# Attention weights turned in 32x32 squares on VectorE and placed by DMA through DRAM, in place of TensorE transposes

## The chip, the cores and the metric

The kernel runs on one core of a Trainium2 chip. The metric is the device time of one execution in microseconds (us), as the median of several runs; lower is better.

## What is computed

Eight batches of causal attention with a window of 128 keys and a linear distance bias, followed by a feed-forward layer with a squared Relu:

```python
B, H, S, D = 8, 8, 576, 64
scores = (q @ k^T) / sqrt(D)                     # per batch and head
rel = pos[:, None] - pos[None, :]
mask = (rel >= 0) & (rel < 128)
scores = where(mask, scores - slope[h] * abs(rel), -1e9)
attn = softmax(scores)                           # divided by (sum + 1e-9)
x = (attn @ v) as [4608 tokens, 512]             # heads side by side
h = maximum(x @ w_in, 0)                         # w_in 512 x 2048
out = (h * h) @ w_out                            # w_out 2048 x 512
```

Inputs and output are float32.

## The kernel before

The 4608 tokens are cut into nine chunks of 512. A chunk's attention has eight **segments**: four pairs of heads times two halves of 256 tokens. Segment k belongs to chunk k // 8, to the pair of heads k // 2 % 4 and to half k % 2. A segment's weights stand in a tile `t` of 128 x 4 x 128: 128 partitions are two blocks of 64 queries, the middle index m is a head and a half of the segment, and the last one is a ring of 128 keys.

The feed-forward layer of a chunk has 16 steps f. In each, `gemm1` (line 169) makes 128 hidden rows by 12 matmuls into one PSUM bank `g`, ScalarE takes the Relu (line 178) into `r`, VectorE squares it (line 184), ScalarE rounds it to `hh` (line 186) and VectorE keeps the rest in `hl` (line 188); two steps later `gemm2` (line 199) adds 12 more matmuls into four accumulators `acc`. There is one buffer of `r` and one bank of `g`.

The first two chunks' attention, and the first GEMM, are laid out by `start` with a planner. From segment 18 on, two segments (a **couple**, q = 9 to 35) are handled together, and the GEMMs of the chunk before run between their parts. TensorE's order is the order in which the code is written. The loop at line 702 counts half steps t (even: gemm1, odd: gemm2), and a couple has 8 of them:

- at part 0 the couple before is finished by `both` (line 352): two times 16 matmuls of weights with values (`mix`, line 335) into one bank, split into high and low parts `xu` by ScalarE and VectorE (lines 359 and 360). The next couple's loads of qk and v are put on SyncE's queue. Then `front`: the couple's scores (line 414), the copy and the mask (lines 441 to 464), the row's maximum (276), the exponential (283), sums and reciprocal (290, 291), and the normalisation on GpSimd (294).
- at parts 3 and 5 `middle` turns one segment each: `turn` has four TensorE transposes of 128 x 128 against the identity into PSUM (line 302), `out` copies them to `own` (ScalarE, line 309), and `before` and `same` make from it, by a select on GpSimd, the part of the ring that belongs to earlier keys (`prev`, line 312) and that of the same block (`own`, line 318).

`own` and `prev` are the two halves of one buffer of the pool `pp`, which has two buffers, so a couple fills both, and a new one is free when the couple before has been mixed. Segments 16 and 17 (couple 8) are scored and normalised in `start`; segment 16 is turned there too, segment 17 in the loop. All engines but TensorE get their order from a scheduler that simulates the program. Each engine, and SyncE's queue with the loads and stores, works through its own list in order.

Of the kernel before, what the change touches and what calls it, by code (L numbers as in the profile page):

```python
# [9 lines left out]
F32 = mybir.dt.float32  # L10
# [4 lines left out]
ALU = mybir.AluOpType  # L15
# [31 lines left out]
class Kern:  # L47
    def __init__(self, ctx, tc, qkd, vd, w1d, w2d, cstd, outd):
        self.tc, self.nc = tc, tc.nc
        self.qkd, self.vd = qkd, vd  # L50
        self.w1d, self.w2d, self.cstd, self.outd = w1d, w2d, cstd, outd
        ep = lambda name, bufs, **kw: ctx.enter_context(tc.tile_pool(name=name, bufs=bufs, **kw))
        self.c = ep("const", 1)
        self.ld = ep("ld", 3)
        self.tp = ep("tp", 3)
        self.pp = ep("pp", 2)
        self.sm = ep("sm", 6)
        self.xu = ep("xu", 8)
        self.hp = ep("hp", 3)
        self.op = ep("op", 4)  # L60
        self.sc = ep("sc", 1, space=PSUM)
        self.at = ep("at", 1, space=PSUM)
        self.g1 = ep("g1", 1, space=PSUM)
        self.ac = ep("ac", 4, space=PSUM)
        self.cst = self.c.tile([128, CST], F32, name="cst")
        self.ident = self.cst[:, 0:128]
        self.mask = self.cst[:, 128:192].bitcast(I32)
        self.never = self.cst[:, 192:256]
        self.raw, self.w = [None] * NF, [None] * NF
        self.nc.alloc_sbuf_tensor("arena", [128, NF * 2048], F32)  # L70
        self.arena = self.nc.sbuf_base - NF * 8192
        self.x, self.qk, self.v, self.h, self.segs = {}, {}, {}, {}, {}
        at = lambda slot, name, shape: self.nc.alloc_sbuf_tensor_at(name, shape, F32, offset=self.arena + slot * 4096).ap()
        self.wide = [at(2 * (NF - 3), "wide", [128, H, 256])[:, 2 * p : 2 * p + 2] for p in range(NP)]
        self.room_t = [at(2 * (NF - 5) + n, f"tw{n}", [128, 4, 256]) for n in range(4)]
        self.start_banks = [self.ac.tile([128, 512], F32, name="acc") for _ in range(4)]
# [138 lines left out]
class Segment:  # L215
# [133 lines left out]

    def both(self, other):
        K = self.K
        X = K.at.tile([128, 512], F32, name="at")
        for s in (self, other):
            s.X = X[:, 256 * s.sg : 256 * s.sg + 256]
            s.mix(s.sg == 0)
        u = K.x[self.c, self.p] = K.xu.tile([128, 2, 512], F32R, name="xu")
        self.nc.scalar.copy(u[:, 0], X)
        self.nc.vector.tensor_tensor(u[:, 1], X, u[:, 0].bitcast(F32), op=ALU.subtract)  # L360
# [5 lines left out]
        self.sums()  # L366
        self.norm()

    def middle(self):
        self.turn()  # L370
        self.out()
        self.before()
        self.same()


class Couple:
# [218 lines left out]
def start(K):  # L595
# [31 lines left out]
    for k in range(18):  # L627
        G = K.segs[k] = (Wide if k < 8 else Segment)(K, k)
        c, p, sg = G.c, G.p, G.sg
        n = lambda s, *m: (s, k, *m)  # L630
        after = [("q", c, p, 0), ("q", c, p, 1)][: sg + 1] + ([("s", k - 1)] if k else []) + LATER * (k == 8)
        chain = lambda s: ((s, k - 1),) if k else ()
        if k < 8:
            d, slot, w = 4.0 * k, "sa" if k % 2 else "sc", 0.75 if G.skip else 1.0
            P.add(n("s"), "PE", 0.9 * w, tuple(after), d, G.scores, slot)
            for m in range(4):
                P.add(n("u", m), "DVE", 0.35 * w, (n("u", m - 1) if m else n("s"), ("k", p)), d + 0.5, do(G.top, m), None if m else "tw", slot if m == 3 else None)
                P.add(n("e", m), "Activation", 0.48 * w, (n("u", m),) + ((n("e", m - 1),) if m else ()), d + 0.5, do(G.exp, m))
            P.add(n("r"), "DVE", 0.4, (n("e", 3),), d + 1, G.sums)
            P.add(n("n"), "Pool", 2.05 * w, (n("r"),), d + 1, G.norm)  # L640
            P.add(n("z"), "PE", 0.9 * w, (n("n"),) + chain("z"), d + 1, G.turn, ("at", "zp", "pp"), "tw")
            P.add(n("o"), "Activation", 0.6, (n("z"),), d + 1, G.out, None, "at")
            P.add(n("m"), "DVE", 0.62 if w == 1 else 0.36, (n("z"),), d + 1, G.also, None, "zp")
            P.add(n("x"), "PE", 1.0, (n("m"), n("o"), ("v", c, p)) + chain("x"), d + 2, G.values, "xa", "pp")
            P.add(n("h"), "Activation", 0.4, (n("x"),), d + 2, G.high)
            P.add(n("l"), "DVE", 0.36, (n("h"),), d + 2, G.low, None, "xa")
        else:
            d = RING(k)
            P.add(n("s"), "PE", 0.9, tuple(after), d, G.scores, "sc")
            P.add(n("b"), "Activation", 0.6 if not G.late else 0.8, (n("s"),), d, G.base, "t")  # L650
            P.add(n("f"), "DVE", 0.7 if not G.late else 1.1, (n("b"),), d, G.fold, None, "sc")
            for m in range(4):
                P.add(n("t", m), "DVE", 0.22, (n("t", m - 1) if m else n("f"), "nrel"), d + 0.5, do(G.top, m))
                P.add(n("e", m), "Activation", 0.4, (n("t", m),) + ((n("e", m - 1),) if m else ()), d + 0.5, do(G.exp, m))
            P.add(n("r"), "DVE", 0.4, (n("e", 3),), d + 1, G.sums)
            P.add(n("n"), "Pool", 1.05, (n("r"),), d + 1, G.norm)
            if k > 16:
                continue
            P.add(n("z"), "PE", 0.55, (n("n"),) + chain("z"), d + 1, G.turn, ("at", "pp"), "t")
            P.add(n("o"), "Activation", 0.6, (n("z"),), d + 1, G.out, None, "at")  # L660
            P.add(n("p"), "Pool", 0.72, (n("o"),), d + 1.5, G.before)
            P.add(n("m"), "Pool", 0.66, (n("p"),), d + 1.5, G.same)
            if k > 15:
                continue
            P.add(n("x"), "PE", 1.1, (n("m"), ("v", c, p)) + chain("x"), d + 2, G.values, "at", "pp")
            P.add(n("h"), "Activation", 0.4, (n("x"),), d + 2, G.high)
            P.add(n("l"), "DVE", 0.36, (n("h"),), d + 2, G.low, None, "at")
        if sg == 1:
            P.add(n("ld"), "free", 0.0, (n("x"),), d + 2, None, None, None if (c, p) == (0, 3) else "ld")
# [24 lines left out]
@with_exitstack  # L694
def tile_attn_moe(ctx: ExitStack, tc: tile.TileContext, *aps):
    K = Kern(ctx, tc, *aps)
    K.const()
    with tc.manual_schedule(engines={ENGINES["PE"]}):
        with tc.manual_schedule(engines={e for n, e in ENGINES.items() if n != "PE"}):
            start(K)  # L700
        pairs = {8: (K.segs[16], K.segs[17])}
        for n in range(NF, NF * NCH + 2):
            for t in (2 * n, 2 * n + 1):
                q, part = divmod(t - FIRST, 8)
                q += 9
                with tc.high_priority(offset=50):
                    if part == 0:
                        if q - 1 in pairs:
                            first, second = pairs.pop(q - 1)
                            first.both(second)  # L710
                        if q + 1 < 4 * NCH:
                            K.load(*divmod(q + 1, 4))
                        if q < 4 * NCH:
                            C = Couple(K, q)
                            C.front()
                            pairs[q] = C.both
                    if part in (3, 5) and q in pairs:
                        pairs[q][part // 4].middle()
                if t % 2 == 0 and n < NF * NCH:
                    for _ in K.gemm1(*divmod(n, NF)):  # L720
                        pass
                if t % 2:
                    K.gemm2(*divmod(n - 2, NF))
# [50 lines left out]
```

## Time and profile before

| what | value |
|---|---|
| median of three runs | 997.27 us (996.41 to 997.94) |
| the profiled execution | 996.04 us |
| its span | 994.2 us |
| TensorE clock granted in it | 0.998 |
| DMA moved | 61.50 MB, mean 62 GB/s |
| transposes of line 302 | 256, in 64 groups of four |
| mixes of line 335 into `at` | 1024 matmuls |

A row of a group of instructions reads: line, engine, operation, tiles written and read, shapes and count, then busy us and mean ns of one, then the idle time of the engine just before them and what ended it. A row of the chain in order of time reads: start, length, engine, tile and line. A timeline row has start and length, engine, line and operation. In the view of waits a row has who waited for whom, the total, the times and the longest. DMA rows have the size of one and the median us from issue to landing. PE is TensorE, PEld its weight loads, DVE VectorE, ACT ScalarE, POOL GpSimd and SP SyncE.

### The profile page before, as it was taken

The page shows a single profiled execution, that of the slowest core. Times are in us where ns is not written, and L with a number is a line of the kernel's source. Part 1 is how long each engine was busy: PE and PEld are TensorE (multiplying, and loading weights), DVE is VectorE, ACT ScalarE, POOL GpSimd, SP SyncE. Part 2 cuts the span into 40 slices and gives each one's busy share as a digit, 9 for nine tenths or more (in the row PEclk, how much of TensorE's full clock was granted, in tenths as well). Part 3 has the DMA queues.
Part 4 walks back from the last instruction along what each step waited for, and adds up shares of the span by engine and source line. Part 5 has one row for each costly group of instructions (what it writes and reads, how often), then busy time and mean ns, then how long its engine had stood idle before and what let it go on. Part 6 is the DMA issues. An engine that isn't in the chain of part 4 may idle for free.

```text
span 994.2 us, 16896 instructions
## 1 busy us (share of the span) xinstructions
PE 984.2 (99%) x6545; PEld 814.1 (82%) x6548; DVE 438.4 (44%) x1269; ACT 453.7 (46%) x1180; POOL 191.8 (19%) x252
## 2 busy tenths in 40 slices
PE   9899999999999999999999999999999999999998
PEld 5678788888888888888888888888888888888886
DVE  6889824444443434344444344333434444422222
ACT  7899744444433444344444343334444444422221
POOL 4132321221112222222212211122222221100000
PEclk9999999999999999999999999999999999999999
DMA  9971202111211002111211121110111110001001
GB/s 350 404 276 53 63 14 80 38 39 38 80 38 39 26 20 73 39 38 38 81 38 38 38 80 38 38 39 19 65 35 39 38 57 1 1 1 43 1 1 42
DMA packets 26943, 61.50 MB, mean 62 GB/s; under 512 B 2928, under 2 KB 4336, under 8 KB 26864
## 3 DMA queue, kind: packets, MB, share of 16 engines
q1 hardware_dynamic: 26432, 59.91, 17.4%
q8 instruction: 51, 0.84, 0.3%
q10 hardware_dynamic: 432, 0.52, 0.2%
q14 instruction: 28, 0.23, 0.1%
HBM read 50.99 MB, written 9.44 MB: 61 GB/s over the span
## 4 chain that ended last, share of the span: by engine, by line
PE 97%; DVE 1%; ACT 1%; issue 0%; POOL 0%; DVEq 0%; POOLq 0%; ACTq 0%
PE acc L199 41%; PE g L169 40%; PE at L335 6%; PE at L302 3%; PE s L414 2%; PE g L414 2%; PE g L105 1%; PE s L239 1%; PE acc L335 1%; PE at L530 0%; PE s L498 0%; PE acc L498 0%; PE acc L533 0%; DVE tw L508 0%; ACT w L155 0%
## 5 line engine op out<-in xcount | busy, mean ns | idle before, releaser
L169 PE MATMUL g<-xu,w 128*128 128x512 f32 x1728 | 433.9, 400 | 2.6 <-ACT r L178 2.6
L199 PE MATMUL acc<-hh,w 128*128 128x512 f32 x1152 | 388.7, 398 | 0.0
L169 PEld LDWEIGHTS g<-xu,w 128*128 128x128 f32 x1728 | 333.3, 196 | 65.3 <-ACT r L178 3.3
L199 PEld LDWEIGHTS acc<-hh,w 128*128 128x128 f32 x1152 | 224.8, 195 | 46.1 <-issue 1.5
L184 DVE TENSOR_TENSOR r<-r 128x512 f32<-128x512 f32 x128 | 88.6, 692 | 342.3 <-ACT r L178 340.4
L199 PE MATMUL acc<-hl,w 128*128 128x512 f32 x576 | 227.6, 395 | 0.0
L178 ACT ACTIVATE r<-g 128x512 f32<-128x512 f32 x144 | 85.5, 594 | 299.5 <-PE g L169 299.2
L188 DVE TENSOR_TENSOR hl<-r,hh 128x512 fp32r<-128x512 f32 x144 | 102.2, 710 | 108.9 <-ACT hh L186 104.7
L186 ACT CAST hh<-r 128x512 fp32r<-128x512 f32 x144 | 89.2, 619 | 95.0 <-DVE r L184 94.5
L199 PEld LDWEIGHTS acc<-hl,w 128*128 128x128 f32 x576 | 112.5, 195 | 20.4
L294 POOL TENSOR_TENSOR t<-t,nm 128x512 f32<-128x512 f32 x64 | 81.1, 1267 | 239.2 <-DVE nm L291 214.2
L283 ACT ACTIVATE t<-t,nm 128x128 f32<-128x128 f32 x256 | 99.5, 390 | 35.2 <-DVE nm L276 35.0
L312 POOL TENSOR_SCALAR_AFFINE_SELECT pp<-pp 128x512 f32<-128x512 f32 x64 | 43.4, 679 | 185.7 <-ACT pp L309 185.6
L335 PEld LDWEIGHTS at<-pp,v 128*64 128x64 f32 x1024 | 55.2, 137 | 12.7 <-issue 12.0
L335 PE MATMUL at<-pp,v 128*64 128x128 f32 x1024 | 63.8, 276 | 0.0
L309 ACT COPY pp<-at 128x512 f32<-128x512 f32 x72 | 42.1, 584 | 45.5 <-PE at L302 44.5
L276 DVE CUSTOM_DVE_ANT_0 t<-t,cst 128x128 f32<-128x128 f32 x256 | 59.2, 293 | 1.0
L450 POOL MEMSET t<- 64x128 f32 (+1 forms) x35 | 8.1, 232 | 236.3 <-PE g L414 235.9
L460 DVE COPY_PREDICATED t<-cst,s 64x256 f32<-64x256 int32 x85 | 37.8, 445 | 32.4 <-ACT t L448 19.1
L283 ACT ACTIVATION_READ_ACCUMULATOR t<-t,nm 128x1 f32 x256 | 48.0, 187 | 0.0
L318 POOL TENSOR_SCALAR_AFFINE_SELECT pp<-pp 128x512 f32<-128x512 f32 x64 | 42.3, 661 | 4.4
L414 PE MATMUL s<-qk 64*64 64x64 f32 (+2 forms) x988 | 40.2, 253 | 0.0
(71 smaller groups left out, 587.4 us busy)
## 6 DMA issues: line engine op xcount, KB each, us to landing
raw<-in_dram SPq DMA_DIRECT2D x32, 512.0 KB, 8.9
qk<-in_dram SPq DMA_DIRECT2D x32, 320.0 KB, 3.5
v<-in_dram SPq DMA_DIRECT2D x32, 320.0 KB, 3.0
qk<-in_dram SPq DMA_DIRECT2D x38, 256.0 KB, 3.8
out_dram<-o SPq DMA_DIRECT2D x35, 256.0 KB, 2.7
v<-in_dram SPq DMA_DIRECT2D x3, 256.0 KB, 5.0
wide<-in_dram SPq DMA_DIRECT2D x3, 256.0 KB, 5.2
qk__200<-in_dram SPq DMA_DIRECT2D x2, 256.0 KB, 5.6
```

Source lines behind the costliest of these rows:

```text
L169: nc.tensor.matmul(g, w[:, cc * 128 : cc * 128 + 128], xs[cc][:, part], start=i == 0, stop=i == 11)
L178: nc.scalar.activation(r, g, AF.Relu)
L184: nc.vector.tensor_tensor(r, r, r, op=ALU.mult)
L186: nc.scalar.copy(hh, r)
L188: nc.vector.tensor_tensor(hl, r, hh.bitcast(F32), op=ALU.subtract)
L199: nc.tensor.matmul(self.acc[m], w[:, ms], h, start=(f == 0 and i == 0), stop=(f == NF - 1 and i == 2))
L276: self.nc.vector.tensor_tensor_reduce(self.t[:, m], self.t[:, m], self.K.nrel(2 * self.p + m // 2), -0.125, BIG, ALU.add, ALU.min, self.nm ...
L283: self.nc.scalar.activation(self.t[:, m], self.t[:, m], AF.Exp, bias=nm[:, m : m + 1], scale=-1.0, accum_out=nm[:, 4 + m : 5 + m],)
L294: self.nc.gpsimd.tensor_tensor(self.t, self.t, self.nm[:, 8:12].unsqueeze(2).to_broadcast([128, 4, 128]), op=ALU.mult)
L312: self.nc.gpsimd.affine_select(self.prev, self.own, pattern=[[0, 4], [-1, 128]], compare_op=ALU.is_gt, fill=0.0, base=0, channel_multiplier=1,
L335: self.nc.tensor.matmul(self.X[r, o : o + 128], v[:, 2 * sg + k, r], src[:, j], start=start and n == 0, stop=n == 3 - self.skip, skip_grou ...
L414: mm = nc.tensor.matmul(to, qk[r, q0 : q0 + 64], qk[r, k0 : k0 + 64 * n], start=True, stop=True, skip_group_check=True,)
```

## The change

From segment 16 on the weights are no longer turned on TensorE. For each segment VectorE transposes `t` in squares of 32 x 32, into the half of the buffer that will be `prev`. That leaves 16 turned squares per 128 x 128 block, each on the partitions of its old row of squares. Four DMAs, one for each 32 partitions, write them to a DRAM tile `way` (64 KB each, in runs of 128 elements), so that row b of squares of the result holds what came from column b; one DMA of 256 KB reads the tile back into `own`. The selects on GpSimd then make `prev` and `own` as before, with a pattern for the new place of the elements. In a partition a weight now stands at (a, m, c), with a and c the query's square and its place there. `mix_squares` does the same 16 matmuls as `mix`, and reads its moving operand as four runs of 32 elements that lie 128 elements apart. Both segments of a couple are turned right behind `front`; segments 16 and 17 right behind `start`. TensorE's transposes, the PSUM tile that they wrote and ScalarE's copy are gone for segments 16 to 71.

```diff
+        self.dr = ep("dr", 4, space=bass.MemoryType.DRAM)
...
+    def turn_squares(self):
+        nc = self.nc
+        self.place()
+        at = lambda x, pattern: x.rearrange("p m c -> p (m c)").rearrange(pattern, m=4, c=32)
+        squares = at(self.prev, "p (b m c) -> p b m c")
+        nc.vector.transpose(squares.rearrange("p b m c -> p m b c"), self.t.rearrange("p m (b c) -> p m b c", c=32))
+        way = self.K.dr.tile([128, 512], F32, name="way")
+        for a in range(4):
+            nc.sync.dma_start(
+                way.rearrange("(b r) (a f) -> a r b f", r=32, a=4)[a],
+                squares[32 * a : 32 * a + 32].rearrange("r b m c -> r b (m c)"),
+            )
+        nc.sync.dma_start(self.own.rearrange("p m c -> p (m c)"), way)
+        self.own, self.prev = (at(x, "p (a m c) -> p a m c") for x in (self.own, self.prev))
+        for to, sign, op in ((self.prev, 1, ALU.is_gt), (self.own, -1, ALU.is_ge)):
+            nc.gpsimd.affine_select(
+                to, self.own, pattern=[[-32 * sign, 4], [0, 4], [-sign, 32]], compare_op=op, fill=0.0,
+                base=0, channel_multiplier=sign,
+            )
+
+    def mix_squares(self):
+        K, sg = self.K, self.sg
+        v = K.v[self.c, self.p]
+        plan = ((0, self.prev, 0, 0), (128, self.prev, 1, 1), (0, self.own, 0, 1), (128, self.own, 1, 2))
+        for n, (o, src, i, k) in enumerate(plan):
+            for j in range(2):
+                r = slice(64 * j, 64 * j + 64)
+                self.nc.tensor.matmul(
+                    self.X[r, o : o + 128].rearrange("p (a c) -> p a c", a=4), v[:, 2 * sg + k, r], src[:, :, 2 * j + i],
+                    start=sg == 0 and n == 0, stop=n == 3, skip_group_check=True,
+                )
...
-            s.mix(s.sg == 0)
+            s.mix_squares()
...
-    def middle(self):
-        self.turn()
-        self.out()
-        self.before()
-        self.same()
...
-            if k > 16:
+            if k > 15:
                 continue
...
+        for s in pairs[8]:
+            s.turn_squares()
...
-                    if part in (3, 5) and q in pairs:
-                        pairs[q][part // 4].middle()
+                            for s in C.both:
+                                s.turn_squares()
```

In the rows below the changed program's lines are one higher up to line 349 (the new pool) and 28 higher behind the new functions.

TensorE, a place in the second half of a couple of the steady part. `acc` is written by gemm2 and `g` by gemm1; `w8`, `w9` and `w11` are the weights of steps 8, 9 and 11, `at` is the PSUM tile of the turned weights, `t` the weights and `cst` the identity. Before:

```order
L199 MATMUL acc_1797<-hh_2109,w8_603 128x512
L302 MATMUL at_2281<-cst_91,t_2201 128x128 x4
L169 MATMUL g_2289<-xu_782,w11_686 128x512 x3
L169 MATMUL g_2289<-xu_1012,w11_686 128x512 x3
L169 MATMUL g_2289<-xu_1234,w11_686 128x512 x3
L169 MATMUL g_2289<-xu_1426,w11_686 128x512 x3
L199 MATMUL acc_1794<-hh_2141,w9_623 128x512
```

The same place in the changed program:

```order
L200 MATMUL acc_1821<-hh_2117,w8_605 128x512
L170 MATMUL g_2308<-xu_784,w11_688 128x512 x3
L170 MATMUL g_2308<-xu_1014,w11_688 128x512 x3
L170 MATMUL g_2308<-xu_1236,w11_688 128x512 x3
L170 MATMUL g_2308<-xu_1428,w11_688 128x512 x3
L200 MATMUL acc_1818<-hh_2149,w9_625 128x512
```

The four transposes between gemm2 and gemm1 are gone, and nothing stands in their place.

VectorE, the end of the softmax of the same couple: sums and reciprocals `nm` of its two segments, then the square of `r` and `hl` of the GEMM that runs meanwhile. Before:

```order
L290 TENSOR_SCALAR nm_2202<-nm_2202 128x4 [waits Activation_49]
L291 RECIPROCAL nm_2202<-nm_2202 128x4 [waits DVE_49]
L290 TENSOR_SCALAR nm_2204<-nm_2204 128x4 [waits Activation_49]
L291 RECIPROCAL nm_2204<-nm_2204 128x4 [waits DVE_49]
L184 TENSOR_TENSOR r_2261<-r_2261 128x512 [waits Activation_49]
L188 TENSOR_TENSOR hl_2263<-r_2261,hh_2262 128x512 [waits PE_49,Activation_49]
```

And in the changed program:

```order
L291 TENSOR_SCALAR nm_2210<-nm_2210 128x4 [waits Activation_49]
L292 RECIPROCAL nm_2210<-nm_2210 128x4 [waits DVE_49]
L291 TENSOR_SCALAR nm_2212<-nm_2212 128x4 [waits Activation_49]
L292 RECIPROCAL nm_2212<-nm_2212 128x4 [waits DVE_49]
L358 STREAM_TRANSPOSE pp_2244<-t_2209 128x4x4x32 [waits DMAHW2_49,DMAHW5_49,DMAHW1_49,DMAHW7_49,DMAHW0_49,Pool_49]
L185 TENSOR_TENSOR r_2289<-r_2289 128x512 [waits Activation_49]
L358 STREAM_TRANSPOSE pp_2254<-t_2211 128x4x4x32 [waits DMAHW4_49,DMAHW6_49,DMAHW3_49,DMAHW7_49,DMAHW0_49,Pool_49]
L189 TENSOR_TENSOR hl_2291<-r_2289,hh_2290 128x512 [waits PE_49,Activation_49]
```

One transpose now stands in front of the square and one in front of `hl`, and each waits for GpSimd's normalisation of its segment (and for DMAs of the buffer's last use). In some couples the first one stands ahead of the second reciprocal.

SyncE's queue of the changed program for the same couple; `way` is the DRAM tile, and before there were only the loads of qk and v in this place (lines 124 and 129) and at a chunk's end the stores of the output:

```order
L125 DMA qk_2653<-in_0_dram 128x512
L361 DMA way_2246<-pp_2244 32x4x128 [waits DVE_49]
L361 DMA way_2246<-pp_2244 32x4x128 [waits DMAHW5_49]
L361 DMA way_2246<-pp_2244 32x4x128 x2
L361 DMA way_2256<-pp_2254 32x4x128 [waits DMAHW0_49,DVE_49]
L361 DMA way_2256<-pp_2254 32x4x128 [waits DMAHW1_49]
L365 DMA pp_2244<-way_2246 128x512 [waits DMAHW5_49,DMAHW6_49,DMAHW4_49,DMAHW7_49,DMAHW2_49,Pool_49]
L361 DMA way_2256<-pp_2254 32x4x128 [waits DMAHW3_49]
L361 DMA way_2256<-pp_2254 32x4x128
L365 DMA pp_2254<-way_2256 128x512 [waits DMAHW3_49,DMAHW1_49,DMAHW4_49,DMAHW0_49,Pool_49]
L130 DMA v_2656<-in_1_dram 128x640 [waits PE_49]
```

Ten DMAs per couple have come between the loads of qk and the next load of v, and the first segment's read back stands behind two writes of the second segment.

More of the change, by code (lines that the diff above doesn't have):

```diff
@@ L662, in start @@
             P.add(n("m"), "Pool", 0.66, (n("p"),), d + 1.5, G.same)
-            if k > 15:
-                continue
             P.add(n("x"), "PE", 1.1, (n("m"), ("v", c, p)) + chain("x"), d + 2, G.values, "at", "pp")
```

## The prediction

> **What bounds the kernel now.** I read the page first (busy shares, then the chain that ended last), then the waits of TensorE, then one stretch of the chain in order of time.
>
> ```profile
> span 994.2 us, 16896 instructions
> PE 984.2 (99%) x6545; PEld 814.1 (82%) x6548; DVE 438.4 (44%) x1269; ACT 453.7 (46%) x1180; POOL 191.8 (19%) x252
> ...
> PE 97%; DVE 1%; ACT 1%; issue 0%; POOL 0%; DVEq 0%; POOLq 0%; ACTq 0%
> PE acc L199 41%; PE g L169 40%; PE at L335 6%; PE at L302 3%; PE s L414 2%; PE g L414 2%; PE g L105 1%; PE s L239 1%; PE acc L335 1%; PE at L530 0%; PE s L498 0%; PE acc L498 0%; PE acc L533 0%; DVE tw L508 0%; ACT w L155 0%
> ```
>
> TensorE is busy for 99% of the span and is 97% of the chain; VectorE, ScalarE and GpSimd are busy for less than half of it. The two GEMMs (lines 199 and 169) are 81% of the chain, the transposes of line 302 are 3%. A busy share can hide waits, so the longest wait of a TensorE matmul, from the view of waits:
>
> ```profile
> PE g L169 <- ACT r L178: 2.6, 1, 2.6
> ```
>
> It is 2.6 us once in the whole run. So what leaves TensorE's queue should leave the span, unless something new makes it wait. One couple of the steady part, from the chain in order of time (start, length, what):
>
> ```profile
> 502.96 1.90 PE at L335 x32
> ...
> 506.22 3.00 PE acc L199 x12
> 509.21 2.80 PE g L169 x12
> 512.01 2.80 PE acc L199 x12
> 514.81 0.44 PE at L302 x4
> 515.25 2.81 PE g L169 x12
> 518.06 2.80 PE acc L199 x12
> 520.86 0.44 PE at L302 x4
> 521.30 2.81 PE g L169 x12
> 524.10 2.80 PE acc L199 x12
> 526.90 2.80 PE g L169 x12
> 529.70 1.90 PE at L335 x32
> ```
>
> The reader is to see that pieces follow each other without a gap: one mix of weights and values (line 335) to the next is 26.74 us, in which the transposes stand twice with 0.44 us, and neighbours without a transpose take the same 2.80 us as those with one.
>
> **The change, part by part.** Removed from TensorE: the transposes of segments 16 to 71, that is 56 groups of four (224 of the 256 that the row below counts; the other 32 belong to segments 8 to 15 and stay).
>
> ```profile
> L302 PE MATMUL at<-cst,t 128*128 128x128 f32 x256 | 38.5, 273 | 0.1
> L309 ACT COPY pp<-at 128x512 f32<-128x512 f32 x72 | 42.1, 584 | 45.5 <-PE at L302 44.5
> L335 PE MATMUL at<-pp,v 128*64 128x128 f32 x1024 | 63.8, 276 | 0.0
> ```
>
> The 273 ns here are the latency of one; the four cost the queue 0.44 us by the chain. 56 x 0.44 = **24.6 us**. At most 0.45 can be read from it (the GEMM behind takes 2.81 and not 2.80), which is 25.2 us. The copies of line 309 leave ScalarE (56 x 0.58 = 33 us), which is not on the chain: no gain.
>
> Added on TensorE: nothing in number. The mix keeps its 32 matmuls per couple, 1.90 / 32 = 59 ns each in the queue. Two things about them are new. Their moving operand is read as four runs of 32 elements, 128 elements apart, where it was one run of 128. No row shows such a moving operand; from below the cost is nothing (the same 128 elements), and not less, since the count stays. From above I take weight loads, the only reads with gaps on this engine:
>
> ```profile
> L169 PEld LDWEIGHTS g<-xu,w 128*128 128x128 f32 x1728 | 333.3, 196 | 65.3 <-ACT r L178 3.3 <-issue 0.6 <-ACT xu L345 0.3
> L302 PEld LDWEIGHTS at<-cst,t 128*128 128x128 f32 x256 | 31.6, 140 | 9.0 <-POOL t L294 1.3
> ```
>
> Line 169 reads every second word (high and low parts lie interleaved) and takes 56 ns longer than line 302, which reads words in a row. If each moving operand paid as much, it were 28 x 32 x 0.056 = 50 us. I take nothing: a gap after each 32 elements is nearer to a plain read than one after every element. The second thing is that four matmuls of a couple now wait for GpSimd and DMA semaphores together. A separate semaphore instruction on this engine took 51 ns:
>
> ```profile
> L302 PEldq EVENT_SEMAPHORE  x34: 51/51/51, 74.8 to 866.0; - x34
> ```
>
> Four for each of 28 couples are at most 5.7 us, and nothing if they are done ahead while the twelve matmuls in front run 2.8 us; the zero idle time in line 335's row, which had such waits too, says nothing, and I take that.
>
> **The round trip that must hide.** Before, the turned weights had only ScalarE's copy and two selects behind them. Now it is VectorE's transpose, four writes to DRAM, a read back, and the two selects, all between the normalisation (line 294) and the next mix. The same couple's timelines:
>
> ```profile
> 512.20 1.04 POOL L294 TENSOR_TENSOR t<-t,nm 128x512 f32<-128x512 f32 x1 [6.13 <-DVE nm L291]
> 513.71 1.55 POOL L294 TENSOR_TENSOR t<-t,nm 128x512 f32<-128x512 f32 x1 [0.47 <-ACT r L178]
> ...
> 522.04 0.64 POOL L312 TENSOR_SCALAR_AFFINE_SELECT pp<-pp 128x512 f32<-128x512 f32 x1 [4.70 <-ACT pp L309]
> 522.75 0.63 POOL L318 TENSOR_SCALAR_AFFINE_SELECT pp<-pp 128x512 f32<-128x512 f32 x1
> ```
>
> ```profile
> 513.38 0.18 DVE L291 RECIPROCAL nm<-nm 128x4 f32<-128x4 f32 x1
> 513.66 0.69 DVE L184 TENSOR_TENSOR r<-r 128x512 f32<-128x512 f32 x1
> 515.04 0.76 DVE L188 TENSOR_TENSOR hl<-r,hh 128x512 fp32r<-128x512 f32 x1 [0.69 <-PE at L302]
> ```
>
> ```profile
> L184 DVE TENSOR_TENSOR r<-r 128x512 f32<-128x512 f32 x128 | 88.6, 692 | 342.3 <-ACT r L178 340.4
> L157 DVE TENSOR_TENSOR w<-raw,w 128x1024 fp32r<-128x1024 f32 x16 | 21.5, 1344 | 1.9 <-ACT w L155 1.5
> ```
>
> ```profile
> 506.26 0.82 SPq L124 DMA_DIRECT2D qk<-in_dram  x2
> ```
>
> ```profile
> v<-in_dram SPq DMA_DIRECT2D x32, 320.0 KB, 3.0
> ...
> v<-in_dram SPq DMA_DIRECT2D x3, 256.0 KB, 5.0
> ...
> out_dram<-o SPq DMA_DIRECT2D x1, 128.0 KB, 2.0
> ```
>
> No row shows a VectorE transpose. I bound it by 0.69 us (one 128x512 operation) and 1.34 us (twice the elements) and take 0.69. Of the two orders that the program has, the worse one: first transpose 513.4 to 514.1, the second reciprocal behind it to 514.3, second normalisation 514.4 to 515.95, second transpose to 516.7. SyncE issues at 0.41 us each: the first four writes are out at 515.75 and land 2.0 us later (the 128 KB row; these are 64 KB), 517.75; two writes of the second segment go out meanwhile, then the first read back, then the other two writes by 518.95, landing at 520.95; the second read is issued by 521.35 and lands 3.0 us later, 524.35; the two selects (0.64, 0.07 between, 0.63) end at 525.7. The mix comes at 529.70 - 0.88 = 528.82, since TensorE has lost two transposes. **3.1 us are left**, so the trip costs nothing.
>
> What waits behind the new waits: on VectorE the hl of line 188 stands behind the second transpose and starts at 516.7 and not 515.04, ending 517.4. ScalarE's next Relu needs it (one buffer of r):
>
> ```profile
> 518.09 0.60 ACT L178 ACTIVATE r<-g 128x512 f32<-128x512 f32 x1 [2.16 <-PE g L169]
> ```
>
> It comes at 518.09 - 0.44 = 517.65, so it is just not late. With transposes of 1.34 us hl would end near 518.7 and the Relu near 519.3, and the GEMM that needs its bank starts at 521.30 - 0.88 = 520.42: still covered. On SyncE the loads of v stand behind the round trip; the order shows that they wait for TensorE's next mix anyway. On GpSimd only the next couple's work stands behind the selects. The first pair (segments 16 and 17) has a second place: its second transpose waits until segment 15's mix frees a buffer.
>
> ```profile
> 130.72 1.02 PE at L335 x16
> ...
> 154.79 1.90 PE at L335 x32
> ```
>
> That is 131.7, and its mix comes at 154.79: 23 us for a trip of about 9.
>
> **Sum.** The profiled execution took 996.04 us (span 994.2 and 1.8 around it); 996.04 - 24.6 = 971.4. The median shown, 997.27, lies 1.2 above that execution, which gives 972.7 on its scale. I write **972**.
>
> **Rivals.** (1) The round trip is longer than what is left. The 5.0 us row above is from the crowded start; with it for writes and reads the trip grows by 3.0 + 2.0, 1.9 beyond the 3.1. Each of 27 couples pays it: 51 us, 996.04 - 24.6 + 51 = 1022. It ends slower than before as soon as the trip is 3.1 + 24.6 / 27 = 4.0 us longer than I worked out. Against it: a couple's loads are issued by 507.1 (506.26 + 0.82) and land by the 3.0 us row near 510, before the first write goes out at 514.1.
>
> The Trainium skill ("VectorE: DVE Perf Modes", "The three transpose paths") speaks against the change: it calls a plain DMA that transposes by strides 19 times slower than the crossbar's 1309 ns for a 128x128 bf16 block, and its rules give such a block to TensorE. By that, as an estimate from the page, one block were 25 us and the kernel several hundred us slower; but these copies keep runs of 128 floats whole and leave the turning itself to VectorE, so its condition is not met, and no row here shows such a DMA. I give it no chance beyond that of this rival.
>
> (2) The moving operand with gaps slows the mix. At the 56 ns above: 1021.6. It decides from 24.6 / 896 = 27 ns per matmul, which is nearly half of its 59 ns. For it: the mix is on the chain without slack. Against it: runs of 32 words.
>
> (3) A little TensorE time comes back, from semaphores (5.7 us) or a few ns per matmul: 974.5 to 983.
>
> (4) The transposes go and the time stays. For it there is only the possibility that another engine bounds the step at once; a step's Relu, square, hh and hl are 0.60 + 0.69 + 0.62 + 0.76 = 2.7 us (hh from the row below) against 2.80 + 2.80 = 5.6 us of TensorE, so hardly: 996. That the change does not do what it says is excluded by the order of instructions, in which the groups are gone.
>
> ```profile
> L186 ACT CAST hh<-r 128x512 fp32r<-128x512 f32 x144 | 89.2, 619 | 95.0 <-DVE r L184 94.5
> ```
>
> **How the numbers follow.** Forecast (970 to 974.5): 0.78. Rival 3: 0.08. Rival 1: 0.06, half of it between 983 and 995, half slower. Rival 2: 0.06, nearly all slower. Rival 4: 0.02. From 970 to 983 stand 0.86. Faster by over 0.2% (about 2 us, what a measurement of this kernel can tell from no change): 0.90; within: 0.02; slower: 0.08.
>
> **What would show it.** In the changed profile: line 302's successor counts 32; pieces of the chain are 2.80, 2.80 without 0.44 between, and a couple takes 25.86 us; the mix is still 1.90 us (rival 2: longer) and has no idle time before it that ends with a GpSimd select (rival 1: one of some us in each couple); a VectorE transpose takes 0.7 to 1.3 us; a write lands near 2 us and a read near 3. I am wrong if a trip takes over 12.9 us from the end of the second normalisation (528.82 - 515.95), or if the mix's matmuls slow down.

## The result, and the profile after

| | before | after |
|---|---|---|
| median of four runs | 996.84 us (994.99 to 997.94) | 968.12 us (966.54 to 969.67) |
| ratio, 95% interval | | 0.9714 (0.9692 to 0.9736) |
| the profiled execution | 996.04 us | 969.67 us |
| its span | 994.2 us | 967.9 us |
| TensorE clock granted in it | 0.998 | 0.998 |
| DMA moved | 61.50 MB | 90.90 MB |

The kernel became faster by 28.7 us. I had forecast 972 us, a gain of 24.6, with 970 to 983 us as the range: the sign and the mechanism held, and the measured median lies 1.9 us below the range. So the question is where four microseconds more came from.

The page of the changed kernel: busy shares, the chain's shares, the groups of the round trip (transpose, selects) and of the mix, and the two kinds of DMA.

```profile
span 967.9 us, 17114 instructions
PE 958.5 (99%) x6321; PEld 793.3 (82%) x6324; DVE 478.9 (49%) x1325; ACT 422.5 (44%) x1124; POOL 202.6 (21%) x252
...
PE 98%; ACT 1%; DVE 1%; DMA 1%; issue 0%; DVEq 0%; ACTq 0%
...
L368 POOL TENSOR_SCALAR_AFFINE_SELECT pp<-pp 128x512 f32<-128x512 f32 x112 | 90.3, 806 | 200.5 <-DMA way<-pp 112.0
...
L380 PE MATMUL at<-pp,v 128*64 128x128 f32 x896 | 55.1, 276 | 0.0
...
L358 DVE STREAM_TRANSPOSE pp<-t 128x512 f32<-128x512 f32 x56 | 39.8, 710 | 24.4 <-POOL t L295 19.0
...
way<-pp SPq DMA_DIRECT2D x224, 64.0 KB, 1.8
...
pp<-way SPq DMA_DIRECT2D x56, 256.0 KB, 2.7
```

TensorE is still the bound, with 224 matmuls fewer. The new work is where it was expected: VectorE's share rises from 44% to 49%, and GpSimd has idle time that ends with a DMA, but the mix (line 335 before, line 380 now) has none, and its matmul's mean is 276 ns as before. A couple without and one with an effect that I had not forecast, from the chain in order of time (start, length, what):

```profile
492.14 1.90 PE at L380 x32
...
495.40 3.00 PE acc L200 x12
498.40 2.80 PE g L170 x12
501.20 2.80 PE acc L200 x12
...
515.20 2.80 PE g L170 x12
```

```profile
518.01 1.90 PE at L380 x32
...
521.27 2.97 PE acc L200 x12
524.24 2.76 PE g L170 x12
527.00 2.76 PE acc L200 x12
...
540.80 2.75 PE g L170 x12
543.55 1.90 PE at L380 x32
```

The first couple takes 518.01 - 492.14 = 25.87 us, which is the 25.86 forecast. The next takes 543.55 - 518.01 = 25.54: each of its GEMM pieces of 12 matmuls is 0.04 us shorter. So a GEMM matmul has two paces here, 2.80 / 12 = 233.3 ns and 2.76 / 12 = 230 ns, at one granted clock (1.00 in each of these two couples, 0.998 over the execution). The trace of before has both as well, which I hadn't looked for. This is the chain behind the scores of an earlier couple, before the change:

```profile
158.17 2.97 PE acc L199 x12
161.15 2.76 PE g L169 x12
163.91 2.76 PE acc L199 x12
166.66 0.44 PE at L302 x4
167.10 2.81 PE g L169 x12
169.91 2.80 PE acc L199 x12
172.71 0.44 PE at L302 x4
```

The fast pace ends at the first group of transposes. Told by **stretches**, the eight GEMM pieces between one couple's scores and the next mix, from the starts of the GEMM matmuls in the trace (F: a piece at the fast pace, a point: a slow one; time of the first):

```
before                    after
184.86 FFF.....           469.47 ........
452.76 FFF.....           521.20 FFFFFFFF
694.08 FFF.....           804.75 FFFFFFFF
```

Before, 10 of 27 stretches began fast, and each lost the pace at its first transposes; after, 11 of 27 ran fast over all eight pieces. The share of distances between GEMM matmuls at the fast pace (mean of two neighbours below 231.7 ns) was 0.114 before and 0.315 after, the mean distance 232.97 and 232.29 ns.

### The profile page after: what moved, and what is told of

The parts are those of the page before. It is cut to its first block, busy times and chain, and to the rows that moved or that the text cites. A ratio compares the mean times of both kernels' runs of the same rounds, so it can differ in the third digit from the quotient of the medians.

```text
span 967.9 us, 17114 instructions
## 1 busy us (share of the span) xinstructions
PE 958.5 (99%) x6321; PEld 793.3 (82%) x6324; DVE 478.9 (49%) x1325; ACT 422.5 (44%) x1124; POOL 202.6 (21%) x252
## 2 busy tenths in 40 slices
DMA packets 67267, 90.90 MB, mean 94 GB/s; under 512 B 7408, under 2 KB 37488, under 8 KB 67184
## 4 chain that ended last, share of the span: by engine, by line
PE 98%; ACT 1%; DVE 1%; DMA 1%; issue 0%; DVEq 0%; ACTq 0%
PE acc L200 42%; PE g L170 42%; PE at L380 5%; PE s L442 2%; PE g L442 2%; PE at L336 1%; PE s L240 1%; PE acc L336 1%; PE g L106 1%; DMA qk<-in_dram 1%; PE acc L526 0%; PE s L526 0%; PE at L558 0%; PE at L303 0%; PE acc L561 0%; ACT w L156 0%
## 5 line engine op out<-in xcount | busy, mean ns | idle before, releaser
L170 PE MATMUL g<-xu,w 128*128 128x512 f32 x1728 | 427.5, 396 | 2.6 <-ACT r L179 2.6
L170 PEld LDWEIGHTS g<-xu,w 128*128 128x128 f32 x1728 | 337.2, 196 | 68.8 <-ACT r L179 4.2
L185 DVE TENSOR_TENSOR r<-r 128x512 f32<-128x512 f32 x128 | 92.5, 722 | 273.9 <-ACT r L179 273.8
L189 DVE TENSOR_TENSOR hl<-r,hh 128x512 fp32r<-128x512 f32 x144 | 104.8, 728 | 86.1 <-ACT hh L187 84.7
L368 POOL TENSOR_SCALAR_AFFINE_SELECT pp<-pp 128x512 f32<-128x512 f32 x112 | 90.3, 806 | 200.5 <-DMA way<-pp 112.0
L295 POOL TENSOR_TENSOR t<-t,nm 128x512 f32<-128x512 f32 x64 | 74.8, 1168 | 249.5 <-DVE nm L292 237.7
L380 PEld LDWEIGHTS at<-pp,v 128*64 128x64 f32 x896 | 48.3, 137 | 10.0 <-issue 10.0
L380 PE MATMUL at<-pp,v 128*64 128x128 f32 x896 | 55.1, 276 | 0.0
L358 DVE STREAM_TRANSPOSE pp<-t 128x512 f32<-128x512 f32 x56 | 39.8, 710 | 24.4 <-POOL t L295 19.0
L442 PEld LDWEIGHTS s<-qk 64*64 64x64 f32 x988 | 36.4, 133 | 0.0
```

The lines of the kernel that those rows point to most:

```text
L170: nc.tensor.matmul(g, w[:, cc * 128 : cc * 128 + 128], xs[cc][:, part], start=i == 0, stop=i == 11)
L185: nc.vector.tensor_tensor(r, r, r, op=ALU.mult)
L189: nc.vector.tensor_tensor(hl, r, hh.bitcast(F32), op=ALU.subtract)
L295: self.nc.gpsimd.tensor_tensor(self.t, self.t, self.nm[:, 8:12].unsqueeze(2).to_broadcast([128, 4, 128]), op=ALU.mult)
L368: nc.gpsimd.affine_select(to, self.own, pattern=[[-32 * sign, 4], [0, 4], [-sign, 32]], compare_op=op, fill=0.0, base=0, channel_multiplie ...
L380: self.nc.tensor.matmul(self.X[r, o : o + 128].rearrange("p (a c) -> p a c", a=4), v[:, 2 * sg + k, r], src[:, :, 2 * j + i], start=sg == ...
```

## The experiments

**Theory P**: the transposes cost their queue time and also end the fast pace; **theory Q**: queue time alone, and the rest is spread between executions. The runs of the first four are compared with the same runs of the kernel before (996.18 us).

| run | median us | ratio to before (95%) | share fast | mean distance, ns |
|---|---|---|---|---|
| four idle transposes | 995.83 | 0.9989 (0.9978 to 1.0) | 0.075 | 233.11 |
| one idle transpose | 976.99 | 0.9813 (0.9798 to 0.9827) | 0.137 | 232.90 |
| the changed kernel again | 969.21 | 0.9732 (0.9716 to 0.9748) | 0.313 | 232.29 |
| trip doubled, one run | 1014.37 | | 0.249 | 232.51 |

**Four idle transposes** put back into TensorE's queue:

```diff
+                    if part in (3, 5) and q in pairs:
+                        z = K.at.tile([128, 4, 128], F32, name="at")
+                        for m in range(4):
+                            K.nc.tensor.transpose(z[:, m % 4], K.ident, K.ident)
```

> The changed kernel, with four TensorE transposes of the identity into a PSUM bank that nobody reads put back at the two places of each couple where the weights' transposes stood (56 groups); everything else is the changed kernel's. Theory Q (queue time alone): each group costs its 0.44 us and nothing else, 968.1 + 24.6 = 992.7 us; the GEMM pieces keep the changed kernel's mixture of 2.76 and 2.80 us (mean distance of GEMM matmuls 232.3 ns, 0.3 of them at the fast distance). Theory P (queue time and pace): a group also ends the fast pace of the GEMM behind it, so pieces of 2.76 us end at the first group of a couple; mean distance 233.0 ns, share near 0.1, and 996 to 997 us, the time of the kernel before.

Measured: 995.83 us, 26.6 more than the changed kernel beside it. There are 55 groups (segment 16 was turned in `start`), so Q's own sum is 55 x 0.44 = 24.2 us. The other 2.4 stand in the pace: 233.11 - 232.29 ns over some 3,300 distances is 2.7 us. Its chain is like that of before, with the idle transposes at line 750:

```profile
485.35 2.76 PE acc L200 x12
488.11 0.44 PE at L750 x4
488.55 2.82 PE g L170 x12
491.37 2.81 PE acc L200 x12
```

All four stretches that began fast became slow at the first group. Nothing else of the change was undone, and the time of before is back: VectorE, GpSimd and the 29 MB more of DMA cost nothing that can be measured. By the times alone P and Q lie only 2.4 us apart, little more than their intervals; the chain and the share part them.

**One idle transpose** in place of four:

> As the run before, with one idle transpose in place of four at each of the 56 places. Theory Q: 56 x 0.11 = 6.2 us, 974.3 us, pace as in the changed kernel (mean distance 232.3 ns). Theory P, if the interruption alone ends the fast pace: 6.2 + 3 = 977 to 978 us, mean distance 233.0 ns, share of fast distances near 0.1. Theory P, if it takes the length of four: the pace stays and the time is Q's.

```profile
477.62 2.76 PE acc L200 x12
480.38 0.11 PE at L750
480.49 2.82 PE g L170 x12
483.31 2.80 PE acc L200 x12
```

976.99 us, 7.8 more than the changed kernel beside it: 55 x 0.11 = 6.1, and (232.90 - 232.29) ns over 3,300 distances, 2.0. A single transpose of 0.11 us ends the fast pace as four do; so it is the interruption and not its 0.44 us. All ten stretches that began fast lost the pace so; one idle transpose, at another couple, also began a fast pace that the next one ended. P again.

**The changed kernel again:**

> The changed kernel once more, for a second sample of the pace: 968 us, ratio to before 0.971. If the pace is set by the program (which couple it is), the same couples run fast and the share of fast GEMM distances is again 0.3; if it is chance, other couples and another share, and the times of its executions spread by as much as the share does (up to 7 us between none and all fast).

969.21 us and a share of 0.313, but other couples: here the stretches at 338.63 to 415.55 ran fast, which were slow in the first profile, and those at 544.32 to 622.21 slow, which were fast. Two more profiles of the same kernel gave shares of 0.222 and 0.203 (967.86 and 968.00 us). In these two the same seven stretches ran fast throughout, and six of them did in the first profile too. So the program alone doesn't fix which stretch runs fast, though much of it repeats. The share is higher than before in each: the four executions of the changed kernel lie at 0.20 to 0.32, the three with them (before and the two runs above) at 0.08 to 0.14.

**The trip doubled**, for my first rival:

```diff
+        again = self.K.dr.tile([128, 512], F32, name="again")
+        nc.sync.dma_start(again, self.own.rearrange("p m c -> p (m c)"))
+        nc.sync.dma_start(self.own.rearrange("p m c -> p (m c)"), again)
```

> The changed kernel, with a second plain write to DRAM and read back of each segment's turned weights behind the first (112 more copies of 256 KB in whole rows, two more issues per segment). The trace of the changed kernel has a median of 2.2 us (least 0.9) between the end of a couple's last select and its mix. If that slack is what hides the trip (my rival 1), a trip longer by 0.41 + 2 + 2.7 = 5 us per segment (up to 7 with both segments' issues in one queue) makes TensorE wait 3 to 5 us before each of 27 mixes: 968 + 80 to 135 = 1050 to 1100 us, slower than before. If transfers are not what ends last there, under 975 us.

The waits of TensorE, and one round of the chain (its mix is line 383, its selects line 371):

```profile
PE at L383 <- POOL pp L371: 27.4, 27, 2.8
```

```profile
485.56 0.66 PE at L383 x8
...
502.96 2.62 DMA pp<-way
505.60 2.30 DMA again<-pp
507.91 2.74 DMA pp<-again
...
510.94 1.22 POOL pp L371
...
512.22 0.74 POOL pp L371
513.00 0.66 PE at L383 x8
```

1014.37 us: slower than before, as the rival has it, but by less than the 1050 to 1100 expected. The chain shows why. It leaves TensorE and goes round through scores, softmax, DMA and selects; in this round the last eight matmuls of the mix start at 485.56 and again at 513.00, so the couple takes 27.44 us instead of 25.87. The slack of 2.2 us, counted against a trip that grows by 2.30 + 2.74 = 5.0 us, should give 2.8 per couple; it gives 1.6. The slack is counted to the start of the mix, but only its last eight of 32 matmuls need the last select, and 24 / 32 of the 1.90 us, 1.4, can be done before it. The rounds differ: from the first GEMM matmul of one couple to that of the next they take 25.9 to 30.6 us, on average 27.7. Some lose nothing, and the five of 29.7 us and more each have 3.4 us at a granted clock of 0.5, behind the five longest waits in the mix (1.7 to 2.8 us). The direction and the place are shown, in one execution; the size was overstated.

**What sets the pace.** The first run put one idle matmul of the identity in front of each GEMM piece, with 8, 32, 64, 96, 128, 192 or 256 columns in turn; the second cut one matmul of each piece in two by columns instead, which adds no work.

```diff
+                if part > 1 or q not in pairs:
+                    z = K.at.tile([128, 512], F32, name="at")
+                    N = SIZES[turn % len(SIZES)]
+                    turn += 1
+                    K.nc.tensor.matmul(z[:, 0:N], K.ident, K.cst[:, 0:N], start=True, stop=True)
```

> The changed kernel, with one idle matmul of the identity with 8, 32, 64, 96, 128, 192 or 256 columns (in turn) in front of each GEMM piece of 12 matmuls behind the third of a couple, and in the part behind the last couple (some 200 pieces in all). It asks what sets the pace of the piece behind an interruption. Theory phase (the interruption's length sets at which point the next weight load meets the running matmul, and that sets the pace): some sizes leave nearly always a fast piece behind them (230 ns per matmul), others hardly ever. Theory chance: about the same share for every size, 0.05 to 0.3. The time is not the question: 968 + 200 x 0.03 to 0.25 us, 985 to 1000.

The cut, in place of the piece's second matmul:

```diff
-        nc.tensor.matmul(out, w, x, start=start, stop=stop)
+        nc.tensor.matmul(out[:, 0:at], w, x[:, 0:at], start=start, stop=False, skip_group_check=True)
+        nc.tensor.matmul(out[:, at:512], w, x[:, at:512], start=False, stop=stop, skip_group_check=True)
```

> The changed kernel, with the second matmul of each GEMM piece (12 matmuls of 512 columns, behind the third chunk's first couple) cut in two by columns: the first 32, 64, 128, 256, 384, 448 or 480 columns (in turn), then the rest. No work is added but one weight load and one matmul per piece. Since a 64-column idle matmul left a fast piece behind it 29 times of 29 or more in the run before, and other sizes hardly ever, a cut should do so too for some of its sizes, if it is the place in time at which the next weight load meets the running matmul that sets the pace: nearly all of that size's pieces at 230 ns, nearly none of the others. If it needs the idle matmul's own weights, no size does. The time: each cut costs 0.03 to 0.1 us, 250 of them 8 to 25 us: 975 to 993.

Pieces at the fast pace behind each size, from the starts of the matmuls:

```
idle columns      8     32     64     96    128    192    256
fast           1/30   0/30  29/29   2/29   0/29   1/29   1/29
cut at           32     64    128    256    384    448    480
fast           2/37  37/37   3/37   0/37   1/36   3/37   2/36
```

The pace isn't chance: 64 columns always left a fast piece. The times, 1029.68 and 988.13 us, were not the question (the first was expected at 985 to 1000, with 0.03 to 0.25 us for an idle matmul; in its chain each stands as two matmuls with 0.12 to 0.43 us). But the order of sizes was fixed, so 64 always followed 32; size and forerunner weren't told apart.

I then tried to use it, with one cut of 64 per couple, at the second matmul behind the scores (first output block of `gemm2`, `m == 0`) and, next, at the eighth (`m == 2`):

```diff
-                    K.gemm2(*divmod(n - 2, NF))
+                    K.gemm2(*divmod(n - 2, NF), 64 if part == 0 and q <= 4 * NCH else 0)
```

> The changed kernel, with one cut per couple: the second matmul of the GEMM piece behind the scores is done as 64 and 448 columns. The run before left 37 of 37 pieces behind such a cut at 230 ns per matmul, for 88 ns more at the cut. If the pace then holds until the next mix, all 28 stretches run fast (0.31 of the distances in the changed kernel): 27 x (0.69 x 96 x 3.3 ns - 88 ns) = 3.5 us, and 468 x 3.3 ns - 88 ns = 1.5 us in the stretch behind the last couple: 968.5 - 5 = 963.5 us, share of fast distances over 0.9 behind the third couple, ratio to before 0.967. If the pace doesn't hold, or the cut at this place doesn't set it: 968.5 + 2.5 = 971.

> The run with one cut per couple, with the cut (64 and 448 columns) at the eighth matmul of the piece behind the scores in place of the second. In that run the cut stood one matmul behind the scores, where the distance before it is 342 to 351 ns and differs from couple to couple, and 5 of 28 stretches became fast; in the run of sizes the matmuls before a cut ran at a steady 233 ns, and 37 of 37 became fast. Theory phase: here the distance before the cut is a steady 233 ns again, so nearly every slow stretch becomes fast from the cut to the next mix (88 matmuls per couple, 460 at the end): 968.2 - 27 x (0.7 x 88 x 3.3 - 88) ns - 1.4 = 964.2 us, ratio to before 0.967, share of fast distances 0.9 (less if a cut that meets a fast stretch makes it slow, which no run shows yet). Rival: only the cut's neighbours matter, not the pace before it: 5 of 28 as before, 970.6 us.

Both missed: 970.61 us (0.9739, 0.9724 to 0.9754) and 973.20 us (0.977, 0.9757 to 0.9783), with 5 of 28 stretches fast behind the cut in each. At the eighth matmul the five were those that came in fast; a slow stretch stayed slow. So 64 columns alone don't do it. The state that the 32 left may have had its part; no run puts the 64 behind another size. Beside the first of them the unchanged after-kernel ran at 967.86 us:

> The changed kernel on the same chip as the run with one cut per couple, for comparison: 968 to 969.5 us, ratio to before 0.971 to 0.973, share of fast distances about 0.3 (by the theory that the phase sets it, any share is possible, since it depends on some ns at each entry).

So I asked which size turns a stretch that has run undisturbed, with the same cut at the eighth matmul of the pieces at parts 1, 4 and 6 and fourteen sizes in turn:

> The changed kernel, with the eighth matmul of every second or third GEMM piece cut in two, the first part 96, 128, 160, 192, 224, 256, 288, 320, 352, 384, 400, 416, 432 or 448 columns in turn (some 100 cuts). In the run of sizes the 64 cut always stood behind a 32 cut, so the fast pace behind it can belong to the pair; one 64 cut in a steady slow stretch left it slow. Here each size meets a stretch that has run undisturbed for 20 matmuls or more. Theory phase: what follows is fixed by the size and the pace before it, so a size that turns a slow stretch fast does so each time it meets one. If no size does, a slow stretch can't be left by one cut. The time: 968 + 100 x 0.003 to 0.05 us, 968 to 973.

The seven cuts of 400 in order of time:

```
cut at 400, pace before:  233  233  230  233  233  233  233 ns
            pace behind:  230  230  233  230  230  230  230 ns
```

No other size did so each time; 256, for instance, sent seven slow stretches through some eight matmuls of 230 to 242 ns, behind which the pace was 233 again. The run took 975.53 us, where 968 to 973 was expected: a cut costs 2 to 90 ns by its size. One cut of 400 per couple, at the eighth matmul of the second piece, beside the changed kernel:

```diff
-                    for _ in K.gemm1(*divmod(n, NF)):
+                    for _ in K.gemm1(*divmod(n, NF), 400 if part == 1 and q <= 4 * NCH else 0):
```

> The changed kernel, with one cut per couple (400 and 112 columns) at the eighth matmul of the second GEMM piece behind the scores. In the run before, a cut of 400 in a steady slow stretch left a fast one behind it 6 times of 6, for 4 ns, and the one that met a fast stretch left 232.8 ns. Theory phase: of 27 stretches about 0.7 come slow and turn fast for their last 76 matmuls, and 0.3 come fast and go to 232.8: 27 x (0.7 x 76 x 3.2 - 0.3 x 76 x 2.8) ns = 2.9 us, and 450 x 3.2 ns = 1.4 us behind the last couple: about 4 us less than the changed kernel, 964 us, share of fast distances 0.65 to 0.75. If single cuts don't carry over to another place: 968.

> The changed kernel on the same chip as the run with cuts of 400, for comparison: 967 to 970 us, ratio to before 0.970 to 0.974; share of fast distances 0.2 to 0.35.

One couple of it, the cut at lines 167 and 168, GEMM matmuls at line 165:

```profile
441.74 3.00 PE acc L165 x12
444.75 1.63 PE g L165 x7
446.38 0.18 PE g L167
446.56 0.05 PE g L168
446.62 0.98 PE g L165 x4
447.60 2.76 PE acc L165 x12
```

All 21 stretches that came at 233 ns went to 230.0 at the cut, and all 7 that came at 230.0 went to 233 ns (the 232.8 of my expectation is a mean that holds the first matmuls behind the cut, which take 226 to 236), as the theory says; the share rose to 0.561, against 0.203 in the run beside it. The time did not follow: 967.67 us (0.9704, 0.9691 to 0.9718) against 968.00 (0.9711, 0.9697 to 0.9724), which can't be told apart.

In the profiles the part from the first such couple to the last became 0.66 us shorter, and the part behind the last one 1.43 (the 1.4 expected); the start was 1.67 longer, which differs from run to run. The couples gave less than their 2.9, for two reasons that the trace shows. A cut costs 64 to 70 ns by itself and not the 4 of my sum, 1.8 us in 27 couples: the cut piece above is 2.85 us long, where seven distances of 233.3 ns and five of 230.0 make 2.78. And five other stretches fell back after one or two pieces. Each of the five did so at a `gemm1` piece whose first weight load had waited for ScalarE's Relu, which frees the bank `g`. The clearest one (start, length, what, idle time before):

```profile
269.19 0.78 PEld L165 LDWEIGHTS g<-xu,w 128*128 128x128 f32 x4 [0.29 <-ACT r L185]
```

Such a late load starts 50 to 51 ns behind the end of the Relu. Six loads in fast stretches were late so, and five of them ended the fast pace; behind the 61 that were in time it never ended. The two go together; no run moves a load alone. So there is no version that is shown to beat the changed kernel.

## Why the prediction held, and where it failed

**The bound.** Right: TensorE is 99% busy and 98% of the chain after, and putting its idle transposes back alone brings the time of before back.

**The sum.** This is the step that failed. I priced a group by its own 0.44 us, noted that "neighbours without a transpose take the same 2.80 us as those with one", and set 25.2 us as the most that could be read from it. All three came from one couple (502.96 to 529.70) that happened to run at the slow pace throughout. The removed groups had a second cost, one that doesn't stand in their own row: they ended the fast pace of the GEMM behind. The idle transposes measured it: 26.6 us for 55 groups where queue time gives 24.2, so 24.6 should have been about 27. In the two profiles this can be followed, from the first piece behind the scores of couple 9 (158.17 before, shown above) to that of the last couple. The chain of before:

```profile
855.65 3.00 PE acc L199 x12
```

and of after:

```profile
158.61 3.02 PE acc L200 x12
...
830.60 2.97 PE acc L200 x12
```

That is 697.5 us before and 672.0 after. Of the 25.5 us, 26 couples' groups are 26 x 0.88 = 22.9; the other 2.6 are pace.

What remains to the 28.7 us is 1 to 2 us, of the size by which the gains of the changed kernel differ between its sets of runs (ratios of 0.9707 to 0.9732, 30.0 to 27.0 us). No run assigns it further, and the pace doesn't explain that spread: the set with a share of 0.222 in its profile gained 30.0 us and the one with 0.313 gained 27.0. The range was too narrow below for both reasons: I gave it 1.4 us under the sum, as if the pace were constant and the start the same in each execution.

**The mix with a moving operand in four runs of 32.** I took nothing, with 50 us as the upper end. Right: 1.90 us and 276 ns, as before.

**The semaphores of the mix.** I took nothing, with at most 5.7 us. Right: idle time 0.0 before the mix's matmuls.

**The round trip.** It hides, as worked out. The same couple in the after kernel, its mix at 518.01:

```profile
503.89 1.33 POOL L295 TENSOR_TENSOR t<-t,nm 128x512 f32<-128x512 f32 x1 [1.13 <-DVE nm L292]
505.25 0.71 DVE L358 STREAM_TRANSPOSE pp<-t 128x512 f32<-128x512 f32 x1 [0.94 <-POOL t L295]
...
507.40 0.90 SPq L361 DMA_DIRECT2D way<-pp  x2
...
510.27 0.34 SPq L365 DMA_DIRECT2D pp<-way  x1
...
513.04 1.84 POOL L368 TENSOR_SCALAR_AFFINE_SELECT pp<-pp 128x512 f32<-128x512 f32 x2 [1.47 <-DMA pp<-way]
```

The last select ends at 513.04 + 1.84 = 514.88, which leaves 3.1 us, the figure of the prediction. That it agrees to the tenth is luck, since the parts were off in both directions: a transpose takes 0.71 us (I took 0.69), a write lands in 1.8 (2.0), a read in 2.7 (3.0), and a pair of selects takes 1.5 to 1.8 (1.34). But this couple is one of the easier ones: over the 28 couples the time between the last select and the mix has a median of 2.2 us and a least of 0.9. The trip that I called hidden with 3.1 us to spare was hidden by a third of that at its worst.

**hl behind the second transpose.** Covered, as forecast, but for a rest. TensorE's only matmul that waits for ScalarE's Relu is the one that did before; the weight loads in front of the matmuls show a little more.

```profile
PE g L170 <- ACT r L179: 2.6, 1, 2.6
PEld g L170 <- ACT r L179: 4.2, 6, 3.1
```

The second row was 3.3, 2, 3.1 before, and it is 3.3, 2, 3.0 with the four idle transposes put back. So the Relu that I called "just not late" is late where the 0.44 us in front of `gemm1` are gone: in five couples of the changed kernel's trace the load starts 51 ns behind its end. By the starts of the matmuls this cost 0.3 us in all.

**Rivals.** The doubled trip shows that the first is real: past the slack most couples pay on the chain, and the kernel is slower than before (I had put a trip longer by 5.0 us at 1022 us; it measured 1014). The case didn't occur in the changed kernel. The Trainium skill ("VectorE: DVE Perf Modes", "Rules for kernel authors") gives a 128x128 transpose to TensorE where PSUM will do as its destination. Here the measurement goes the other way: the four transposes of a segment cost 0.44 us on the engine that bounds, and the 0.71 us of VectorE with its detour lie on engines that have time, for a ratio of 0.9714. Rivals 2 and 4 are out by the mix's 1.90 us and by the time; rival 3 saw a few nanoseconds per matmul, but with the wrong sign.

## What to carry to other kernels

When an engine is 99% of the chain, moving small work off it paid its whole queue time here, and what the work did to its neighbours came on top. So before pricing a removal, look at the neighbours' durations over the whole run, not in one period: 2.76 beside 2.80 was there to be seen, and its place, always before the first transposes, said what ended it. A detour on idle engines is sure to be free only up to its least slack over all rounds (0.9 us here), not up to that of the round that one reads.

## What the runs showed of the hardware

- Back-to-back weight load and 512-column matmul, at a granted clock of 1.00, has two steady paces here: 230.0 ns and 233.3 ns. What follows an interruption depends on the interruption's length in columns and on the pace before it: a cut at 400 columns turned 27 of 27 stretches of 233 ns to 230.0 and 8 of 8 of 230.0 ns to 233 (two kernels). Behind some interruptions up to nine matmuls of 226 to 242 ns come first.
- The pace holds until the next interruption, unless a weight load comes late: in the four profiles of the changed kernel and in that with cuts of 400, each of the eight changes inside a stretch (two of them from slow to fast) stands at a load that waited for ScalarE's Relu. That the timing of weight loads sets the pace in general is a guess that no run tests.
- Behind waits of TensorE of 1.7 to 2.8 us inside the mix, five times in the run with the doubled trip, the granted clock fell to 0.5 for 3.4 us.
- A VectorE transpose of 128 x 512 f32 in squares of 32 took 0.71 us, as long as a plain operation of that size (0.69).
- A 64 KB write to DRAM in runs of 128 elements landed 1.8 us after its issue, a 256 KB read in whole rows in 2.7 us.
